# Decode attention over a 512 MiB cache: tiles of two heads with 64 KB runs in a ring of three slots

## The chip, the cores and the metric

The kernel runs on one core of a Trainium2 chip. The metric is the device time of one execution in microseconds (us); lower is better. A ratio is the mean time of one kernel's runs over the mean of the other's runs of the same rounds, so it is not quite the quotient of the medians that stand beside it. "Span" is the time from the first to the last instruction in the profile; it is about 2 us less than the device time.

Engines are named as in the profile: PE is the TensorE matmul, PEld its weight load, DVE is VectorE, ACT ScalarE, POOL GpSimd, SP SyncE. SPq and ACTq are the sequencers that issue DMA loads. "DMA engine" means one of the 16 hardware engines that move the bytes, not a queue.

## The reference, cut to what matters

```
# B=2, one query position, D=1024, H=32 heads, Sk=16384, Dh=128, bf16
g = sigmoid((x * gate_w).sum(-1))
q = x @ wq                                    # (B, H, Dh)
p = softmax(q . k_cache / sqrt(Dh))           # k_cache: (B, H, Sk, Dh), 256 MiB
a = (p . v_cache) @ wo                        # v_cache: 256 MiB
b = a small two-layer MLP branch of x with layernorms (w1, w2, w3, w4)
out = g * a + (1 - g) * b
```

The caches and weights are 572.5 MB (decimal), each byte of which is needed once. There is little arithmetic for each byte: the kernel is a stream of K and V tiles through on-chip memory.

## The kernel before: the parts that matter

Every K or V tile is one (batch, head) pair: 4 MB, 128 partitions with one contiguous run of 32 KB each. Five such slots form a ring. DVE transposes a K tile in eight pieces, PE multiplies them with a zero-padded q and collects scores in PSUM.

```python
big = ctx.enter_context(tc.tile_pool(name="big", bufs=5))      # 4 MB each
tpool = ctx.enter_context(tc.tile_pool(name="tpool", bufs=3))  # K transposed, 128x1024 f32
# ... other pools cut

def load_k(i):
    b, h = pairs[i]
    t = big_tile("Kn")
    nc.sync.dma_start(
        out=t[:].rearrange("p (j d) -> p j d", d=Dh),
        in_=A_k_cache[b, h].rearrange("(p j) d -> p j d", p=P),
    )
    kn_tiles[i] = t

x_pm = const.tile([P, B, KC], BF16)          # x by columns, pieces of 16 bytes
nc.scalar.dma_start(out=x_pm[:], in_=A_x.rearrange("b s (p r) -> p (b s) r", p=P))
x_row = rows.tile([B, D], BF16)
nc.scalar.dma_start(out=x_row[:], in_=A_x.rearrange("b s d -> (b s) d"))
# ... gate_w is loaded to two rows; the gate is computed on two partitions

def qk_stage(i):
    # ... cut
    for m in range(NM):                      # NM = 8
        T = tpool.tile([P, 2, CJ, 32], FP32, name="T")
        nc.vector.transpose(out=T[:].rearrange("p w j s -> p j w s"),
                            in_=Kw[:, m * CW : (m + 1) * CW].rearrange(...))
        for v in range(4):
            nc.tensor.matmul(S[:], lhsT=z[:, v, 7 - m : 7 - m + P],
                             rhs=Tb[:, v // 2, :, v % 2], start=..., stop=...)

# program order: q, gate, ln1, then for each pair: k, v of the pair before, softmax.
# A load is issued on the SP queue once the step that frees its slot has been built:
ring_size = {"big": 5, "wo": 3}
```

Of the kernel before, what the change touches and what calls it, by code (L numbers as in the profile page):

```python
# [10 lines left out]
FP32 = mybir.dt.float32  # L11
# [12 lines left out]
def kernel(  # L24
# [20 lines left out]
    assert Sq == 1 and Dh == P and B == 2  # L45
    NJ = Sk // P
    KC = D // P
    FC = F // P
    NM = 8
    CJ = NJ // NM  # L50
    NC_ = CJ * 32
    assert NC_ <= 512 and NJ == NM * CJ and D % 512 == 0
    scale = float(Dh) ** -0.5
    NPAIR = B * H
    SLOT = NJ * Dh
    W = 512
    DH2 = D // W

    const = ctx.enter_context(tc.tile_pool(name="const", bufs=1))
    big = ctx.enter_context(tc.tile_pool(name="big", bufs=5))  # L60
    tpool = ctx.enter_context(tc.tile_pool(name="tpool", bufs=3))
    wpool = ctx.enter_context(tc.tile_pool(name="wpool", bufs=3))
    ppool = ctx.enter_context(tc.tile_pool(name="ppool", bufs=2))
    stat = ctx.enter_context(tc.tile_pool(name="stat", bufs=3))
    rows = ctx.enter_context(tc.tile_pool(name="rows", bufs=1))
# [3 lines left out]
    mps = ctx.enter_context(tc.tile_pool(name="mps", bufs=3, space=PSUM))  # L69

    def misc_psum(shape, dtype):
        return mps.tile(shape, dtype, tag="misc", name="misc")
# [3 lines left out]


    pairs = [(b, h) for h in range(H) for b in range(B)]

    def load_rows(src, r0, rn, name):  # L80

        N = src.shape[1]
        t = big_tile(name)
        nc.sync.dma_start(
            out=t[:, : rn * N].rearrange("p (r n) -> p r n", n=N),
            in_=src.rearrange("(p r) n -> p r n", p=P)[:, r0 : r0 + rn, :],
        )
        return t[:, : rn * N].rearrange("p (r n) -> p r n", n=N)

# [3 lines left out]
    V_SPLIT_LAST = [NJ // 2, NJ // 4, NJ // 8, NJ // 8]  # L93

    def load_k(i):
        b, h = pairs[i]
        t = big_tile("Kn")
        nc.sync.dma_start(
            out=t[:].rearrange("p (j d) -> p j d", d=Dh),
            in_=A_k_cache[b, h].rearrange("(p j) d -> p j d", p=P),  # L100
        )
        kn_tiles[i] = t

    def load_v(i):
        b, h = pairs[i]
        t = big_tile("Vn")
        tv = t[:].rearrange("p (j d) -> p j d", d=Dh)
        src = A_v_cache[b, h].rearrange("(p j) d -> p j d", p=P)
        j0 = 0
        for n in V_SPLIT_LAST if i == NPAIR - 1 else [NJ]:  # L110
            nc.sync.dma_start(out=tv[:, j0 : j0 + n, :], in_=src[:, j0 : j0 + n, :])
            j0 += n
        vn_tiles[i] = t

    def load_wo(h):
        t = wpool.tile([P, D], BF16, tag="woh", name="woh")
        nc.sync.dma_start(out=t[:], in_=A_wo[h * Dh : (h + 1) * Dh, :])
        wo_tiles[h] = t

    x_pm = const.tile([P, B, KC], BF16)  # L120
    with nc.allow_non_contiguous_dma(reason="4 KB"):
        nc.scalar.dma_start(out=x_pm[:], in_=A_x.rearrange("b s (p r) -> p (b s) r", p=P))
    x_row = rows.tile([B, D], BF16)
    nc.scalar.dma_start(out=x_row[:], in_=A_x.rearrange("b s d -> (b s) d"))
    gw_row = rows.tile([B, D], BF16, tag="tmp_bf")
    for b in range(B):
        nc.scalar.dma_start(out=gw_row[b : b + 1, :], in_=gate_w.rearrange("(o d) -> o d", o=1))


    ident_bf = const.tile([P, P], BF16)  # L130
    make_identity(nc, ident_bf[:])
# [4 lines left out]
    quarter_f = const.tile([P, P], FP32)  # L136
    nc.vector.memset(quarter_f[:], 0.25)
    nscale_f = const.tile([1, P], FP32)
    nc.vector.memset(nscale_f[:], -scale)

    selv = const.tile([P, 4, 4, 32], BF16)
# [12 lines left out]
    own = const.tile([P, 16], BF16)  # L154
    nc.vector.memset(own[:], 0.0)
    for a in range(4):
        nc.vector.memset(own[32 * a : 32 * a + 32, 4 * a : 4 * a + 4], 1.0)

    assert CJ == 16
    osel = const.tile([P, 4], FP32)  # L160
    nc.vector.tensor_copy(out=osel[:], in_=ident_f[:, 0:8:2])
    for g in range(1, 4):
        nc.vector.tensor_tensor(
            out=osel[:], in0=osel[:], in1=ident_f[:, 40 * g : 40 * g + 8 : 2], op=ALU.add
        )
    ZW = P + 8
    NZ = 3
# [8 lines left out]


    pre_row = rows.tile([B, D], FP32)
    g_row = const.tile([B, 1], FP32)
    omg_row = const.tile([B, 1], FP32)  # L180

    def compute_gate():
        prod = pre_row
        nc.vector.tensor_tensor(out=prod[:], in0=x_row[:], in1=gw_row[:], op=ALU.mult)
        z = stat.tile([B, 1], FP32, name="z")
        nc.vector.reduce_sum(out=z[:], in_=prod[:], axis=AX.X)
        th = stat.tile([B, 1], FP32, name="zt")
        nc.scalar.activation(out=th[:], in_=z[:], func=ACTF.Tanh, scale=0.5)
        nc.vector.tensor_scalar(
            out=g_row[:], in0=th[:], scalar1=0.5, scalar2=0.5, op0=ALU.mult, op1=ALU.add  # L190
        )
        nc.vector.tensor_scalar(
            out=omg_row[:], in0=th[:], scalar1=-0.5, scalar2=0.5, op0=ALU.mult, op1=ALU.add
        )


    qT = const.tile([P, H, B], BF16)
    qsel = const.tile([P, NPAIR, 4], BF16)

    def compute_q():  # L200
        q_f = const.tile([P, H, B], FP32)
        for half in range(2):
            qps = misc_psum([P, H, B], FP32)
            rn = KC // 2
            for h in range(H):
                for r in range(rn):
                    nc.tensor.matmul(  # L207
                        qps[:, h, :],
                        lhsT=wq_half[half][:, r, h * Dh : (h + 1) * Dh],
                        rhs=xT[:, half * rn + r, :],  # L210
                        start=(r == 0),
                        stop=(r == rn - 1),
                    )
            if half == 0:
                nc.vector.tensor_copy(out=q_f[:], in_=qps[:])
            else:
                nc.vector.tensor_tensor(out=qT[:], in0=q_f[:], in1=qps[:], op=ALU.add)
        qs_ps = misc_psum([P, 4, NPAIR], FP32)
        for v in range(4):
            nc.tensor.matmul(  # L220
                qs_ps[:, v],
                lhsT=selv[:, v].rearrange("p a w -> p (a w)"),
                rhs=qT[:].rearrange("p h b -> p (h b)"),
                start=True,
                stop=True,
            )
        nc.vector.tensor_copy(out=qsel[:], in_=qs_ps[:].rearrange("p v n -> p n v"))

    def build_z(i):
        if i >= NPAIR:  # L230
            return
        z = z_tiles[i % NZ]
        nc.gpsimd.tensor_tensor(  # L233
            out=z[:, :, 7 : 7 + P].rearrange("p v (x e) -> p v x e", e=8)[:, :, :, 0],
            in0=qsel[:, i, :].unsqueeze(2).to_broadcast([P, 4, 16]),
            in1=own[:].unsqueeze(1).to_broadcast([P, 4, 16]),
# [5 lines left out]
    wo_acc = [acc.tile([B, W], FP32, name=f"wo_acc{n}") for n in range(DH2)]  # L242
# [4 lines left out]
    def qk_stage(i):  # L247
        Kw = kn_tiles.pop(i)[:].bitcast(FP32)
# [3 lines left out]
        CW = CJ * Dh // 2  # L252
        for m in range(NM):
            T = tpool.tile([P, 2, CJ, 32], FP32, name="T")
            nc.vector.transpose(  # L255
                out=T[:].rearrange("p w j s -> p j w s"),
                in_=Kw[:, m * CW : (m + 1) * CW].rearrange("p (j w e) -> p j w e", w=2, e=32),
            )
            Tb = T[:].rearrange("p w j s -> p w (j s)").bitcast(BF16).rearrange(
                "p w (n two) -> p w n two", two=2  # L260
            )
            for v in range(4):
                nc.tensor.matmul(  # L263
                    S[:],
                    lhsT=z[:, v, 7 - m : 7 - m + P],
                    rhs=Tb[:, v // 2, :, v % 2],
                    start=(m == 0 and v == 0),
                    stop=(m == NM - 1 and v == 3),
                )

    def softmax_stage(i):
# [3 lines left out]
        mT = misc_psum([1, P], FP32)  # L275
        nc.tensor.transpose(mT[:], m[:], ident_f[:])
        mx = stat.tile([1, 1], FP32, name="mx")
        nc.vector.reduce_max(out=mx[:], in_=mT[:], axis=AX.X)  # L278
        nb_ps = misc_psum([P, 1], FP32)
        nc.tensor.matmul(nb_ps[:], lhsT=nscale_f[:], rhs=mx[:], start=True, stop=True)  # L280
        nb = stat.tile([P, 1], FP32, name="nb")
        nc.vector.tensor_copy(out=nb[:], in_=nb_ps[:])  # L282
        Pr = ppool.tile([P, NC_], BF16, name="Pr")
# [4 lines left out]
        PT = ppool.tile([P, CJ, 32], BF16, name="PT")  # L288
        nc.vector.transpose(out=PT[:].rearrange("p j m -> p (j m)"), in_=Pr[:])  # L289
# [3 lines left out]
    def pv_rows(V, PT, oc):  # L293
# [4 lines left out]
        for m in range(NM):  # L298
            lhsT = PT[:].rearrange("p j m -> p (j m)")[:, m : CJ * 32 : 16]
            for g in range(4):  # L300
# [3 lines left out]
                    lhsT=lhsT,  # L304
# [4 lines left out]
        Os = rows.tile([P, 4, Dh], FP32, name="Os")  # L309
# [284 lines left out]
```

## Time and profile before

| | |
|---|---|
| device time | 1348.2 us |
| span of the profiled run | 1346.0 us |
| HBM read | 572.5 MB |
| rate from 150 to 1300 us | 430 GB/s |
| 572.5 MB at that rate | 1331 us |

First, lines of the profile's page: the busy time of each engine, the busy tenths of the 16 DMA engines and their GB/s in 40 slices of the span, the queue of instruction fetches (packets, MB, share of the DMA engines), the chain that ended last by engine, and the group of the K transposes (busy us, mean ns | idle before, what ended most of it).

```profile
PE 955.1 (71%) x5716; PEld 452.2 (34%) x5716; DVE 743.6 (55%) x954; ACT 88.4 (7%) x195; POOL 34.4 (3%) x79
...
DMA  9999999999999999999999999999999999999996
GB/s 405 427 431 431 432 429 430 431 430 432 426 430 432 431 429 428 432 433 430 426 433 432 429 429 429 433 429 431 427 429 430 433 428 430 430 433 429 428 431 293
...
q14 instruction: 15, 0.12, 0.0%
...
DMA 61%; PE 26%; DVE 8%; issue 2%; ACT 1%; DVEq 0%; POOL 0%; ACTq 0%
...
L255 DVE STREAM_TRANSPOSE T<-Kn 128x1024 f32<-128x1024 f32 x512 | 596.1, 1216 | 114.7 <-DMA Kn<-in_A_k_cache_dram 89.9
```

No compute engine is near full, DMA is at 9 tenths or more in 39 of 40 slices, and the last chain is mostly DMA. So the kernel is bound by DMA: only the speed of the packets, a gap in their stream, and the head and tail of the run can change the time.

The view of DMA issues (size, us from issue to landing) and the timeline of the start (start us, duration, engine, instruction [idle before it <- what ended it]) show the head:

```profile
x_pm<-in_A_x_dram ACTq DMA_DIRECT2D x1, 4.0 KB, 22.0
```

```profile
22.77 0.17 DVE L175 COPY xT<-x_pm 128x16 bf16<-128x16 bf16 x1 [20.32 <-DMA x_pm<-in_A_x_dram]
...
34.30 9.36 DVE L255 STREAM_TRANSPOSE T<-Kn 128x1024 f32<-128x1024 f32 x8
```

The 4 KB of x take 22 us, because they come in 256 pieces of 16 bytes on the ACT queue while the SP queue streams big packets. The first K transpose begins at 34.3 us. With five slots there is enough in flight to cover that.

The table of windows (window, length, then busy us and count of PE, PEld, DVE, ACT, POOL, then granted clock, DMA share, GB/s) for the start, the middle and the end:

```profile
core 0: us, PE busy (x) PEld busy (x) DVE busy (x) ACT busy (x) POOL busy (x), PEclk, DMA share, GB/s
80.00:92.00 12.00, 8.11 (x25) 3.28 (x26) 8.89 (x9) 0.55 (x2) 0.00 (x0) 0.59 1.00 425
110.00:120.00 10.00, 8.62 (x65) 4.24 (x63) 4.72 (x7) 0.80 (x2) 0.49 (x1) 0.98 0.98 421
150.00:1300.00 1150.00, 829.49 (x4719) 389.37 (x4718) 637.03 (x805) 76.56 (x170) 27.27 (x56) 0.75 1.00 430
1334.00:1338.00 4.00, 2.32 (x15) 1.96 (x16) 1.37 (x5) 0.82 (x3) 0.00 (x0) 0.72 0.56 231
1338.00:1342.00 4.00, 3.69 (x129) 3.52 (x129) 0.23 (x2) 0.00 (x0) 0.00 (x0) 0.50 0.20 76
```

There is no gap at the start, and at the end the share of busy DMA engines falls from full to nothing within about 10 us.

### The profile page before, as it was taken

Reading aid. Unit: us, or ns where it says so; the run is one execution under the profiler, and the core shown is the slowest. Engines: PE = TensorE matmul, PEld = TensorE weight load, DVE = VectorE, ACT = ScalarE, POOL = GpSimd, SP = SyncE. Lnnn points to the kernel's source line nnn. Section 1 sums busy time; section 2 is a strip of 40 time slices with the busy share of each in tenths; the row PEclk is TensorE's granted clock in tenths of the full one; section 3 lists DMA queues with packets and bytes.
Section 4 is the critical chain, followed back from the end, with each engine's and each line's share of the span. In section 5 each row is a group of like instructions: output and inputs, shape, how many; then the busy total and the mean of one; then the engine's idle time right before and its main releaser. Section 6 shows DMA issues by size and latency. Waiting matters only on the chain.

```text
span 1346.0 us, 13528 instructions
## 1 busy us (share of the span) xinstructions
PE 955.1 (71%) x5716; PEld 452.2 (34%) x5716; DVE 743.6 (55%) x954; ACT 88.4 (7%) x195; POOL 34.4 (3%) x79
## 2 busy tenths in 40 slices
PE   2777677677767766777667687767766766876776
PEld 2333333333333324333223233333333333333333
DVE  2756546456636653656526536655655665664564
ACT  0000000000000000000000000000000000000000
POOL 0000000000000000000000000000000000000000
PEclk9887677778877776887778778778777777777877
DMA  9999999999999999999999999999999999999996
GB/s 405 427 431 431 432 429 430 431 430 432 426 430 432 431 429 428 432 433 430 426 433 432 429 429 429 433 429 431 427 429 430 433 428 430 430 433 429 428 431 293
DMA packets 24967, 573.39 MB, mean 426 GB/s; under 512 B 3014, under 2 KB 3014, under 8 KB 7372
## 3 DMA queue, kind: packets, MB, share of 16 engines
q1 hardware_dynamic: 24628, 572.54, 99.3%
q8 instruction: 44, 0.72, 0.2%
q14 instruction: 15, 0.12, 0.0%
q10 hardware_dynamic: 280, 0.01, 0.0%
HBM read 572.53 MB, written 0.00 MB: 425 GB/s over the span
## 4 chain that ended last, share of the span: by engine, by line
DMA 61%; PE 26%; DVE 8%; issue 2%; ACT 1%; DVEq 0%; POOL 0%; ACTq 0%
DMA Kn<-in_A_k_cache_dram 37%; DMA Vn<-in_A_v_cache_dram 22%; PE S L263 14%; DVE T L255 6%; PE O L302 5%; PE misc L433 2%; DMA x_pm<-in_A_x_dram 2%; PE misc L312 2%; PE misc L407 1%; ACT Pr L285 1%; DVE PT L289 1%; ACT Os L310 1%; PE misc L207 1%; PE misc L280 0%; PE misc L318 0%
## 5 line engine op out<-in xcount | busy, mean ns | idle before, releaser
L255 DVE STREAM_TRANSPOSE T<-Kn 128x1024 f32<-128x1024 f32 x512 | 596.1, 1216 | 114.7 <-DMA Kn<-in_A_k_cache_dram 89.9
L263 PE MATMUL S<-T,z_136 128*128 128x512 bf16 x704 | 208.6, 458 | 58.4 <-DVE T L255 57.1
L263 PE MATMUL S<-T,z_138 128*128 128x512 bf16 x672 | 199.5, 460 | 66.4 <-DVE T L255 65.8
L263 PE MATMUL S<-T,z_140 128*128 128x512 bf16 x672 | 201.7, 465 | 57.7 <-DVE T L255 57.4
L302 PE MATMUL O<-Vn,PT 128*32 128x512 bf16 x2016 | 133.3, 410 | 40.0 <-DMA Vn<-in_A_v_cache_dram 40.0
L337 DVE TENSOR_SCALAR OT<-misc,rinv 128x1 bf16<-128x1 f32 x64 | 14.1, 221 | 246.1 <-PE misc L312 242.6
L263 PEld LDWEIGHTS <-z_136 128*128 128x128 bf16 x704 | 81.7, 116 | 180.3 <-issue 125.7
L263 PEld LDWEIGHTS <-z_138 128*128 128x128 bf16 x672 | 78.7, 117 | 183.5 <-issue 132.7
L263 PEld LDWEIGHTS <-z_140 128*128 128x128 bf16 x672 | 79.3, 118 | 176.4 <-issue 126.4
L302 PEld LDWEIGHTS <-PT 128*32 128x32 bf16 x2016 | 69.9, 143 | 100.5 <-DMA Vn<-in_A_v_cache_dram 48.0
L312 PE MATMUL misc<-osel,Os 128*128 128x1 f32 x504 | 69.6, 259 | 47.2 <-ACT Os L310 47.2
L310 ACT COPY Os<-O 128x512 f32<-128x512 f32 x63 | 36.9, 585 | 994.5 <-PE O L302 994.5
L312 PEld LDWEIGHTS misc<-osel,Os 128*128 128x128 f32 x504 | 64.2, 200 | 78.4 <-ACT Os L310 78.4
L274 DVE TENSOR_REDUCE m<-S 128x1 f32<-128x512 f32 x64 | 44.3, 693 | 74.4 <-PE S L263 74.4
L332 PE MATMUL misc<-rs,quarter_f 128*128 128x1 f32 x128 | 35.8, 349 | 67.0 <-ACT Pr L285 67.0
L289 DVE STREAM_TRANSPOSE PT<-Pr 128x512 bf16<-128x512 bf16 x64 | 45.4, 709 | 50.3 <-ACT Pr L285 50.3
L285 ACT ACTIVATE Pr<-S,nb 128x512 bf16<-128x512 f32 x64 | 44.0, 687 | 224.1 <-DVE nb L282 224.1
L332 PEld LDWEIGHTS misc<-rs,quarter_f 128*128 128x128 f32 x128 | 30.7, 297 | 72.7 <-ACT Pr L285 72.3
L280 PE MATMUL misc<-mx,nscale_f 1*128 1x1 f32 x128 | 28.3, 288 | 13.8 <-DVE mx L278 13.8
L280 PEld LDWEIGHTS misc<-mx,nscale_f 1*128 1x128 f32 x128 | 22.8, 221 | 36.7 <-DVE mx L278 36.7
L282 DVE COPY nb<-misc 128x1 f32<-128x1 f32 x64 | 10.1, 157 | 45.1 <-PE misc L280 45.1
L233 POOL TENSOR_TENSOR z_136<-qsel,own 128x64 bf16<-128x64 bf16 x22 | 10.7, 487 | 431.8 <-PE S L263 424.9
(85 smaller groups left out, 232.1 us busy)
## 6 DMA issues: line engine op xcount, KB each, us to landing
Kn<-in_A_k_cache_dram SPq DMA_DIRECT2D x64, 4096.0 KB, 46.1
Vn<-in_A_v_cache_dram SPq DMA_DIRECT2D x63, 4096.0 KB, 39.3
wt<-in_B_w_dram SPq DMA_DIRECT2D x4, 3584.0 KB
woh<-in_A_wo_dram SPq DMA_DIRECT2D x32, 256.0 KB, 39.0
wq_161<-in_A_wq_dram SPq DMA_DIRECT2D x1, 4096.0 KB, 12.2
wq_163<-in_A_wq_dram SPq DMA_DIRECT2D x1, 4096.0 KB, 21.7
wt<-in_B_w_dram SPq DMA_DIRECT2D x2, 2048.0 KB
Vn<-in_A_v_cache_dram SPq DMA_DIRECT2D x1, 2048.0 KB
```

Source lines behind the costliest of these rows:

```text
L255: nc.vector.transpose(out=T[:].rearrange("p w j s -> p j w s"), in_=Kw[:, m * CW : (m + 1) * CW].rearrange("p (j w e) -> p j w e", w=2, e=32),
L263: nc.tensor.matmul(S[:], lhsT=z[:, v, 7 - m : 7 - m + P], rhs=Tb[:, v // 2, :, v % 2], start=(m == 0 and v == 0), stop=(m == NM - 1 and v ...
L274: nc.vector.reduce_max(out=m[:], in_=S[:], axis=AX.X)
L280: nc.tensor.matmul(nb_ps[:], lhsT=nscale_f[:], rhs=mx[:], start=True, stop=True)
L285: nc.scalar.activation(out=Pr[:], in_=S[:], func=ACTF.Exp, bias=nb[:], scale=scale, accum_out=rs[:])
L289: nc.vector.transpose(out=PT[:].rearrange("p j m -> p (j m)"), in_=Pr[:])
L302: nc.tensor.matmul(O[32 * g : 32 * g + 32, :], lhsT=lhsT, rhs=V[:, j0 : j0 + 4, :], start=(m == 0), stop=(m == NM - 1),)
L310: nc.scalar.copy(out=Os[:].rearrange("p x d -> p (x d)"), in_=O[:])
L312: nc.tensor.matmul(oc[:], lhsT=Os[:, x, :], rhs=osel[:, x : x + 1], start=(x == 0), stop=(x == 3))
L332: nc.tensor.matmul(tot_ps[:], lhsT=quarter_f[:], rhs=rs[:], start=True, stop=True)
L337: nc.vector.tensor_scalar(out=OT[:, h, b : b + 1], in0=oc[:], scalar1=rinv[:, 0:1], scalar2=None, op0=ALU.mult)
L433: nc.tensor.matmul(dst[n][:], lhsT=actT[:, r0 + r, :], rhs=w[:, r, n * W : (n + 1) * W], start=(first and r == 0), stop=(last and r == rn ...
```

## The change

Its intent is fewer and larger DMA packets: a tile holds two neighbouring heads, so that each partition reads one run of 64 KB. To fit, the ring shrinks from five slots of 4 MB to three of 8 MB, and the buffers for transposed K from three of 128x1024 to two of 128x512. Scores, softmax and outputs work on two heads at once, which halves their number. The gate and the MLP branch work on columns (all 128 partitions) instead of rows. The diff, cut to its core:

```diff
-    big = ctx.enter_context(tc.tile_pool(name="big", bufs=5))
-    tpool = ctx.enter_context(tc.tile_pool(name="tpool", bufs=3))
+    big = ctx.enter_context(tc.tile_pool(name="big", bufs=NBIG))      # NBIG = 3, 8 MB each
+    tpool = ctx.enter_context(tc.tile_pool(name="tpool", bufs=2))
 ...
     def load_k(i):
-        b, h = pairs[i]
         t = big_tile("Kn")
         nc.sync.dma_start(
-            out=t[:].rearrange("p (j d) -> p j d", d=Dh),
-            in_=A_k_cache[b, h].rearrange("(p j) d -> p j d", p=P),
+            out=t[:].rearrange("p (j d) -> p j d", d=Dh), in_=cache_rows(A_k_cache, i)
         )
 ...
     x_pm = const.tile([P, B, KC], BF16)
+    gw_pm = const.tile([P, KC], BF16)
         nc.scalar.dma_start(out=x_pm[:], in_=A_x.rearrange("b s (p r) -> p (b s) r", p=P))
-    x_row = rows.tile([B, D], BF16)
-    nc.scalar.dma_start(out=x_row[:], in_=A_x.rearrange("b s d -> (b s) d"))
-    gw_row = rows.tile([B, D], BF16, tag="tmp_bf")
-    for b in range(B):
-        nc.scalar.dma_start(out=gw_row[b : b + 1, :], in_=gate_w.rearrange("(o d) -> o d", o=1))
+        nc.scalar.dma_start(out=gw_pm[:], in_=gate_w.rearrange("(p r) -> p r", p=P))
 ...
     def compute_gate():
-        prod = pre_row
-        nc.vector.tensor_tensor(out=prod[:], in0=x_row[:], in1=gw_row[:], op=ALU.mult)
+        prod = const.tile([P, B, KC], FP32, name="prod")
+        nc.vector.tensor_tensor(
+            out=prod[:], in0=x_pm[:], in1=gw_pm[:].unsqueeze(1).to_broadcast([P, B, KC]), op=ALU.mult
+        )
 ...
         for m in range(NM):                                  # NM: 8 -> 16, for two heads
-            T = tpool.tile([P, 2, CJ, 32], FP32, name="T")
-            nc.vector.transpose(... whole, 128x1024 ...)
-            for v in range(4):
-                nc.tensor.matmul(...)
+            for wh in range(2):
+                T = t_tile([P, CJ, 32], FP32)
+                nc.vector.transpose(out=T[:], in_=Kw[:, m * CJ : (m + 1) * CJ, wh, :])
+                for par in range(2):
+                    nc.tensor.matmul(...)
 ... softmax of two heads at once, output of two heads at once, MLP by columns: cut ...
-    ring_size = {"big": 5, "wo": 3}
+    ring_size = {"big": NBIG, "wo": 1, "T": G}
```

One thing that the diff alone does not show is the order of DVE's instructions. DVE runs its program in order. In the built kernel the copy of x, then `prod` (which waits for the gate load `gw_pm`), come ahead of the copies of q that the scores need and ahead of the first K transposes. And DVE's program grows from 1344 to 2373 instructions, counted in the built programs with the register and semaphore instructions that the profile does not count: two half transposes stand where one whole one stood.

## The prediction

> **What bounds the kernel now.** DMA. The slice row shows the 16 DMA engines at 9 tenths or more in 39 of 40 slices, 430 GB/s inside (the window table: 430 GB/s and a DMA share of 1.00 from 120 to 1300 us). The kernel reads 572.5 MB, 1331 us at that rate; the rest of the 1346 us span is a 2 us start, a 6 us tail after the last V piece, and slower ends. PE (71%) and DVE (55%) are not the limit: in the chain of waits most of the time is K and V loads.
>
> **What the change does.** Same bytes. K and V packets of 64 KB instead of 32 KB (a row per partition is now one run). In the packet records a 32 KB packet takes 1216 ns (median), 16 KB 614 ns: about 12 ns fixed plus the bytes. Halving 16,512 packets on 16 engines saves an estimated 6 to 10 us, if a 64 KB run really is one packet. Softmax and output work, halved in count, is off the critical path. w4 by columns costs PE 224 loads and matmuls of about 60 ns for 56 of about 300: the same.
>
> **What it puts at risk: the ring.** Three 8 MB slots instead of five of 4 MB.
> 1. Start. The x load is 16-byte pieces on another queue, 16 per DMA engine. In the timeline it lands only at 22 us: in the packet records, one 16-byte packet passes after each 1.22 us K packet. The Trainium skill (DMA: Bandwidth & Descriptors, Queues, rings and completion order) says that an engine round-robins between queues by packet; this trace agrees. With 64 KB packets (estimate 2.42 us) x lands at about 42 us and the new gate load behind it, 8 pieces per engine, at about 63. The built order of DVE puts the gate product, which waits for it, before the copies that lead to q and before the first K transposes. So they start near 66 us (34 before). K0's slot comes free near 93, but the DMA queue (wq, K0, K1, V0) ran dry at 80; V1 waits likewise for K1. Estimate: 10 to 15 us idle twice, before K2 and before V1.
> 2. Pace. A half transpose is about 0.71 us (128x512 bf16: 709 ns). With two T buffers each pair of buffers costs transpose + two matmuls + about 0.1 us: 0.71 us per half at full clock, 0.93 at half (granted clock mean 0.76), so 26 to 27 us for K's 32 halves, 4.5 for outputs, 5.5 for the softmax chain: 37 of the 39.5 us that the DMA needs per K and V. It holds, with little to spare.
> 3. Tail about the same (5 to 7 us).
>
> **Sum:** 1348 - 8 + 25 (start) - 1 to + 4 = about 1364 us, 1343 to 1388. Faster by 2% is impossible in practice (the DMA floor is above 1321): 0.01. Within 2%: 0.76. Slower by 2%: 0.23.
>
> **What the profile would show.** Right: packets of 65536 B near 2.42 us; 432 to 433 GB/s in middle slices; x landing near 42 us, the first transpose near 66; two dips of DMA in the third and fourth slices, DMA at 9 tenths after. Transposes of about 0.7 us.
>
> **What would make it wrong.** If runs are cut into 32 KB packets, x lands at 22 us, gate at 33, no start stall and no saving: 1346 to 1352. If small packets don't wait longer behind large ones, the saving stays: about 1340. If the work per tile exceeds 39.5 us, each of 32 tiles adds the excess, and it goes beyond 1390.

## More of the kernel before

Runs e1 to e9 were made on three chips (e1 to e4, e5 to e7, and e8 with e9). The kernel before ran beside each group, with medians of 1348.53, 1348.25 and 1348.10 us, so a difference between runs of different groups is uncertain by about 0.4 us. The lines of the profile's page shown in this section are those of the kernel before.

## The result, and the profile after

| | before | after |
|---|---|---|
| device time, median of 4 runs | 1348.18 us | 1369.95 us |
| lowest and highest | 1348.01, 1348.26 | 1369.56, 1370.39 |
| ratio, 95% interval | | 1.0162 [1.0144, 1.0179] |
| rate from 150 to 1300 us | 430 GB/s | 431 GB/s |

All outputs are right. The changed kernel is 1.6% slower. That is within the 2% that count as "same" here, but the 21.8 us are real: the four runs of each kernel here lie within 0.9 us of each other.

Lines of the page of the changed kernel, the same as shown of before:

```profile
PE 901.4 (66%) x5707; PEld 401.5 (29%) x5770; DVE 783.3 (57%) x1373; ACT 45.0 (3%) x99; POOL 14.3 (1%) x45
...
DMA  9967999999999999999999999999999999999995
GB/s 422 434 280 336 428 426 430 434 426 438 426 436 434 434 425 434 428 432 436 435 430 432 434 432 430 432 428 432 430 434 427 431 428 429 432 426 434 431 414 230
...
q14 instruction: 23, 0.18, 0.0%
...
DMA 53%; PE 26%; DVE 16%; another core or an unknown queue 2%; issue 2%; ACT 1%; SPq 0%; ACTq 0%
...
L284 DVE STREAM_TRANSPOSE T<-Kn 128x512 f32<-128x512 f32 x1024 | 688.3, 701 | 220.6 <-DMA Kn<-in_A_k_cache_dram 152.7
```

DMA has two dips, in the third and fourth slice (280 and 336 GB/s), and is full from then on. So the kernel is still bound by DMA, but with a gap near the start. The last slice is also emptier than before (230 against 293 GB/s).

The small loads in the view of DMA issues (other issues left out), and the timeline from the start to the second gap, with one line of the tail:

```profile
x_pm<-in_A_x_dram ACTq DMA_DIRECT2D x1, 4.0 KB, 41.4
...
gw_pm<-in_gate_w_dram ACTq DMA_DIRECT2D x1, 2.0 KB, 61.7
```

```profile
42.12 0.17 DVE L195 COPY xT<-x_pm 128x16 bf16<-128x16 bf16 x1 [39.85 <-DMA x_pm<-in_A_x_dram]
...
63.01 0.17 DVE L213 TENSOR_TENSOR prod<-x_pm,gw_pm 128x16 f32<-128x16 bf16 x1 [20.71 <-DMA gw_pm<-in_gate_w_dram]
...
65.93 1.30 DVE L284 STREAM_TRANSPOSE T<-Kn 128x512 f32<-128x512 f32 x2
...
89.54 0.33 SPq L97 DMA_DIRECT2D Kn<-in_A_k_cache_dram  x1
...
117.49 0.33 SPq L108 DMA_DIRECT2D Vn<-in_A_v_cache_dram  x1
...
1362.62 0.59 PE L350 MATMUL misc<-PT,Vn 128*128 128x2 bf16 x16 [0.48 <-DMA Vn<-in_A_v_cache_dram]
```

x lands at 42 us, the gate weights at 63 us, and only then can DVE go on to q and to the first transpose at 65.9 us (34.3 before). The slot of the first K tile is free when its last transposes are done, so the third K tile (L97) is issued at 89.5 us; the second V tile (L108) waits likewise for the second K tile, until 117.5 us. The waits of the DMA queue between 30 and 135 us say the same (us in total, times, longest):

```profile
SPq L97 <- DVE T L284: 36.9, 1, 36.9
...
SPq L108 <- DVE T L284: 27.5, 1, 27.5
```

The windows, as for before, and at the end of the run:

```profile
80.00:92.00 12.00, 9.00 (x31) 2.92 (x30) 9.93 (x17) 0.00 (x0) 0.33 (x1) 1.00 0.26 88
110.00:120.00 10.00, 8.97 (x60) 3.51 (x62) 7.63 (x12) 0.00 (x0) 0.34 (x1) 1.00 0.29 105
150.00:1300.00 1150.00, 783.03 (x4663) 344.87 (x4717) 679.89 (x1171) 38.69 (x86) 10.83 (x30) 0.82 1.00 431
1350.00:1354.00 4.00, 1.99 (x18) 1.63 (x16) 1.03 (x5) 1.08 (x3) 0.00 (x0) 0.97 0.53 205
1354.00:1358.00 4.00, 2.82 (x92) 2.85 (x93) 0.99 (x3) 0.18 (x2) 0.00 (x0) 0.50 0.06 27
1358.00:1362.00 4.00, 4.00 (x156) 4.00 (x153) 0.00 (x0) 0.00 (x0) 0.00 (x0) 0.50 0.10 29
```

Two things are to be seen. First, the two gaps: DMA is busy for a quarter of the windows at 80 and 110 us that were full before. Summed over the packet records from 20 to 200 us, the DMA engines are idle for 18.35 us. Secondly, the tail: from 1354 us on the DMA share is 0.06, which is one engine of 16. One DMA engine goes on alone until 1362 us, and the last matmuls wait for what it brings.

The packet records (each packet's start, duration, queue and bytes, which the trace holds beside its views) give the two other quantities of the argument:

| packet | count | median ns | mean ns |
|---|---|---|---|
| before, 32768 bytes | most of K and V | 1216 | 1220 |
| after, 65536 bytes | 8192 | 2420 | 2432 |

Two packets of 32 KB take 2440 ns, one of 64 KB 2432: about 8 ns less. That is little, and the rate in the middle of the run rose only from 430.1 to 431.0 GB/s by those records. And while the big packets stream, sixteen 16-byte packets, as many as there are DMA engines, pass in every 2.42 us now and in every 1.22 us before: one for each big packet. The Trainium skill ("DMA: Bandwidth & Descriptors", section "Queues, rings and completion order") says that a DMA engine serves its queues in turn, a whole packet at a time; this trace agrees, with the intervals just given. The page typically counts 9 to 17 descriptors to a packet; here a turn of the small queue was a single piece of 16 bytes.

### The profile page after: what moved, and what is told of

It is laid out like the page before. It is cut to its first block, busy times and chain, and to the rows that moved or that the text cites. A ratio compares the mean times of both kernels' runs of the same rounds, so it can differ in the third digit from the quotient of the medians. Undisturbed runs are those within 1.5% of the kernel's fastest.

```text
span 1367.8 us, 14339 instructions
## 1 busy us (share of the span) xinstructions
PE 901.4 (66%) x5707; PEld 401.5 (29%) x5770; DVE 783.3 (57%) x1373; ACT 45.0 (3%) x99; POOL 14.3 (1%) x45
## 4 chain that ended last, share of the span: by engine, by line
DMA 53%; PE 26%; DVE 16%; another core or an unknown queue 2%; issue 2%; ACT 1%; SPq 0%; ACTq 0%
DMA Kn<-in_A_k_cache_dram 46%; PE S L289 19%; DVE T L284 15%; PE O L333 4%; DMA Vn<-in_A_v_cache_dram 4%; DMA x_pm<-in_A_x_dram 3%; PE misc L343 1%; PE wo_acc L379 1%; ACT Os L341 1%; PE misc L200 1%; ACT Pr L317 0%; DVE PT L321 0%; DVE OT L371 0%; DVE mx L310 0%
## 5 line engine op out<-in xcount | busy, mean ns | idle before, releaser
L284 DVE STREAM_TRANSPOSE T<-Kn 128x512 f32<-128x512 f32 x1024 | 688.3, 701 | 220.6 <-DMA Kn<-in_A_k_cache_dram 152.7
L289 PE MATMUL S<-T,z_135 128*128 128x512 bf16 x992 | 328.4, 419 | 142.9 <-DVE T L284 130.9
L289 PE MATMUL S<-T,z_137 128*128 128x512 bf16 x993 | 325.2, 414 | 144.7 <-DVE T L284 131.8
L289 PEld LDWEIGHTS <-z_135 128*128 128x128 bf16 x1024 | 107.0, 104 | 361.4 <-issue 308.1
L289 PEld LDWEIGHTS <-z_137 128*128 128x128 bf16 x1024 | 106.4, 104 | 360.1 <-issue 305.9
L343 PE MATMUL misc<-osel,Os 128*128 128x2 f32 x248 | 32.7, 254 | 12.6 <-ACT Os L341 11.2
L431 PEld LDWEIGHTS <-wt 128*128 128x128 bf16 x576 | 35.9, 169 | 16.4 <-DMA wt<-in_B_w_dram 15.1
L321 DVE STREAM_TRANSPOSE PT<-Pr 128x512 bf16<-128x512 bf16 x32 | 22.7, 711 | 28.7 <-ACT Pr L317 28.7
L343 PEld LDWEIGHTS misc<-osel,Os 128*128 128x128 f32 x248 | 30.0, 191 | 21.1 <-ACT Os L341 21.1
L300 DVE TENSOR_REDUCE m<-S 128x1 f32<-128x512 f32 x32 | 22.2, 692 | 22.5 <-PE S L289 22.5
L317 ACT ACTIVATE Pr<-S,nb 128x512 bf16<-128x512 f32 x32 | 22.0, 688 | 122.1 <-DVE nb L312 119.1
L379 PEld LDWEIGHTS <-woh 128*128 128x128 bf16 x256 | 20.7, 168 | 10.4 <-issue 10.2
L237 PEld LDWEIGHTS <-wt 128*128 128x128 bf16 x256 | 7.1, 104 | 45.0 <-DMA wt<-in_A_wq_dram 22.7
```

The lines of the kernel that those rows point to most:

```text
L237: nc.tensor.matmul(qps[:, h, :], lhsT=wq[:, r, h * Dh : (h + 1) * Dh], rhs=xT[:, r, :], start=(r == 0), stop=(r == KC - 1),)
L284: nc.vector.transpose(out=T[:], in_=Kw[:, m * CJ : (m + 1) * CJ, wh, :])
L289: nc.tensor.matmul(S[:], lhsT=z[:, 2 * wh + par, NM - 1 - m : NM - 1 - m + P], rhs=Tb[:, :, par], start=(m == 0 and wh == 0 and par == 0), ...
L300: nc.vector.reduce_max(out=m[:], in_=S[:], axis=AX.X)
L317: nc.scalar.activation(out=Pr[:], in_=S[:], func=ACTF.Exp, bias=nb[:], scale=scale, accum_out=rs[:])
L321: nc.vector.transpose(out=PT[:], in_=Pr[:])
```

## The experiments

The theory that the prediction leaves: the late start (small loads behind 64 KB packets, with DVE in order behind them) costs some 20 us, and the larger packets give some back. Rivals: the two small transpose buffers are too slow for the pace all along; the loss is in the tail; or the larger packets themselves give nothing. The first four runs separate these.

### e1: the small loads first

The loads of x and of the gate weights are issued on the SP queue, ahead of all the big loads.

```diff
-        nc.scalar.dma_start(out=x_pm[:], in_=A_x.rearrange("b s (p r) -> p (b s) r", p=P))
-        nc.scalar.dma_start(out=gw_pm[:], in_=gate_w.rearrange("(p r) -> p r", p=P))
+        nc.sync.dma_start(out=x_pm[:], in_=A_x.rearrange("b s (p r) -> p (b s) r", p=P))
+        nc.sync.dma_start(out=gw_pm[:], in_=gate_w.rearrange("(p r) -> p r", p=P))
```

> The changed kernel with the two small loads (x and the gate weights) issued first on the queue of the big loads. Theory (late start behind 64 KB packets): both small loads land by about 4 us, q starts when wq has landed (about 23 us), the first K transpose at about 34 us, no DMA gap before K2 or V1; 18.7 us of idle DMA vanish, so about 1351 us. Rival (the ring of three 8 MB slots cannot feed the DMA however early it starts): gaps of over 5 us stay, 1360 us or more.

Measured: 1351.66 us, ratio to before 1.0024 [1.0009, 1.0039]. The view of DMA issues has x landing 1.7 us after its issue; the first transpose begins at 44.4 us, when the first K tile has landed. The window that had the first gap, two of the tail, and the page's line of instruction fetches:

```profile
80.00:92.00 12.00, 10.13 (x34) 3.27 (x34) 11.85 (x18) 0.00 (x0) 0.00 (x0) 1.00 0.99 427
1334.00:1338.00 4.00, 1.32 (x20) 1.16 (x21) 1.65 (x6) 0.78 (x2) 0.00 (x0) 0.78 0.20 81
1338.00:1342.00 4.00, 4.00 (x156) 4.00 (x154) 0.00 (x0) 0.00 (x0) 0.00 (x0) 0.50 0.08 30
```

```profile
q14 instruction: 22, 0.18, 0.0%
```

The gap is gone and 18.3 us with it, close to the idle time that was measured in the changed kernel (18.35 us). The match is not exact: in its first 20 us e1 has 0.8 us more idle time than the changed kernel (e6 mends that), and it has one fetch of instructions less (see the tail, below). So the late start is most of the loss, and the pace of the transposes is not the matter: with the same two small buffers there is no other gap. But e1 is still slower than before, and the tail with one lone DMA engine (share 0.08 from 1338 us) is still there.

### e2: the gate after the second softmax

The loads stay late; only the gate's work on DVE is moved out of the way of q and the first K tile. (`prod` lies in a shared buffer so that the order is kept.)

```diff
-        prod = const.tile([P, B, KC], FP32, name="prod")
+        prod = ppool.tile([P, B, KC], FP32, tag="PrOs", name="prod")
 ...
-    steps = [("q", compute_q), ("gate", compute_gate)]
+    steps = [("q", compute_q)]
 ...
             steps.append(("", lambda i=i: softmax_stage(i + 1)))
+        if i == 0:
+            steps.append(("gate", compute_gate))
```

> The changed kernel with the gate's work placed behind the second tile's softmax, x still loaded late (about 42 us). Theory: the first K transpose moves from 66 to about 54 us; K0 is used up near 78 us, just before the DMA runs dry at 80.5, so the first gap (10.0 us) vanishes; K1 is used up near 105.5 us while K2 has landed at 100, so a second gap of about 6 to 7 us stays: about 1358 us. If the gate's load has no part in it, 1370.

Measured: 1356.84 us, ratio 1.0063 [1.0046, 1.0079]. The first transpose begins at 53.1 us instead of 65.9. Two windows:

```profile
80.00:92.00 12.00, 9.76 (x29) 3.40 (x29) 9.60 (x17) 1.59 (x3) 0.00 (x0) 0.72 1.02 438
100.00:107.00 7.00, 6.36 (x48) 2.60 (x50) 5.03 (x8) 0.00 (x0) 0.33 (x1) 1.00 0.44 150
```

The first gap is gone, and of the second 5.9 us are left. The gate's place in DVE's program cost 13.1 us (1369.95 less 1356.84), the late x alone 5.2 us (1356.84 less e1's 1351.66). So x itself is late enough to harm a ring of three, and the gate load behind it is the larger part.

### e3 and e4: runs of 32 KB again

Every load with runs of 64 KB is issued as two with runs of 32 KB; e3 from the changed kernel, e4 from e1.

```diff
-        nc.sync.dma_start(
-            out=t[:].rearrange("p (j d) -> p j d", d=Dh), in_=cache_rows(A_k_cache, i)
-        )
+        tk = t[:].rearrange("p (j d) -> p j d", d=Dh)
+        src = cache_rows(A_k_cache, i)
+        for a in range(2):
+            sl = slice(a * NJ // 2, (a + 1) * NJ // 2)
+            nc.sync.dma_start(out=tk[:, sl, :], in_=src[:, sl, :])
 ... the same for V and the weights
```

> The changed kernel with every 64 KB run loaded as two loads of 32 KB runs: same ring, same slots, same order, packets of 32 KB. Theory: x lands near 22 us and the gate load near 33, first K transpose near 36, no gap; the packets cost 2 to 4 us more in all: about 1354 us. Rival (the ring itself): still 1365 or more.

> Both: early x and 32 KB packets. Against the run with early x alone it measures what packets of 64 KB are worth by themselves, with no start stall in either. From the packet records (2 x 1220 ns against 2432 ns, 8192 packets on 16 engines): 4 us slower than with 64 KB packets; if the last engine to finish decides instead, anything within 5 us either way.

Measured: e3 1357.03 us, ratio 1.0064 [1.0049, 1.0079], 3 us more than expected; e4 1357.74 us, ratio 1.0070 [1.0055, 1.0085]. In e3 x, on the ACT queue, lands as early as in the kernel before and the gate weights behind it, as the view of DMA issues shows, and the window has no gap:

```profile
x_pm<-in_A_x_dram ACTq DMA_DIRECT2D x1, 4.0 KB, 22.1
...
gw_pm<-in_gate_w_dram ACTq DMA_DIRECT2D x1, 2.0 KB, 32.5
```

```profile
80.00:92.00 12.00, 10.86 (x88) 4.39 (x87) 8.12 (x12) 0.00 (x0) 0.34 (x1) 1.00 1.02 437
```

So the size of the big packets is what made the small loads late: apart from it, only the number of big loads issued differs between e3 and the changed kernel. With 32 KB packets it makes no odds whether the small loads are early (e4 is 0.7 us slower than e3). And the large packets do give something: e4 is 6.1 us slower than e1, more than the 4 us that the packet durations had led me to expect (8 ns for each of 8192 packets over 16 engines).

What is left: e3 and e4 have neither a gap nor the gain of large packets, and are still some 9 us slower than the kernel before. All four runs have the lone DMA engine at the end.

### The tail: two theories

From the packet records I took, for each kernel, the time at which four or more DMA engines were last busy with packets of 4 KB or more of the cache and weight loads, and the time at which the last such packet ended:

| kernel | fetch packets on q14 | four engines busy until | last packet ends | difference |
|---|---|---|---|---|
| before | 15 | 1339.3 | 1339.8 | 0.5 |
| after | 23 | 1352.5 | 1362.1 | 9.6 |
| e1 | 22 | 1334.6 | 1344.1 | 9.5 |
| e4 | 23 | 1339.8 | 1349.3 | 9.5 |

(The counts of fetch packets are the profile's own; in the changed kernel's, one packet has 96 bytes, so that 22 have 8 KB.) The kernels with half transposes have one DMA engine 9.5 us behind the others. What else is different about them? q14 is a queue of instruction fetches: packets of 8 KB, 325 ns each, one for about every 128 instructions of DVE (1029 more instructions, 8 more packets). At the end of the changed kernel, where the lone engine's packets can be told apart, the records show one such fetch between V packets of 4 KB that otherwise take 160 ns:

| start us | ns | queue | bytes |
|---|---|---|---|
| 1359.55 | 160 | loads | 4096 |
| 1359.70 | 332 | q14, instructions | 8192 |
| 1360.02 | 499 | loads | 4096 |
| 1360.50 | 31 | loads | 4 |
| 1360.52 | 476 | loads | 4096 |
| 1360.99 | 160 | loads | 4096 |

The fetch and the slower packets around it cost that engine about 1.0 us (332 for the fetch, 499 and 476 less the usual 160 each, and some 20 for the packet of 4 bytes). Theory A: DVE's fetches all ride on one DMA engine; eight or nine more of them put it 8 to 9 us behind, and since each tile has rows from every engine, the last tile lands that much later. Theory B: the half transposes make the last K tile slow to finish (22.9 us from its first to its last transpose, in the median tile), and the end of the run waits for that.

### e5: whole transposes again

From e1: transposes of 128x1024 in two buffers of that size. Room is made by keeping the softmax's and the output's scratch tiles in those same buffers, by one z tile instead of two, and by loading the last two `wo` tiles into a big slot. DVE's program falls from 2373 to 1317 instructions.

```diff
-            for wh in range(2):
-                T = t_tile([P, CJ, 32], FP32)
-                nc.vector.transpose(out=T[:], in_=Kw[:, m * CJ : (m + 1) * CJ, wh, :])
+            T = t_tile([P, 2, CJ, 32], FP32)
+            nc.vector.transpose(
+                out=T[:].rearrange("p w j s -> p j w s"), in_=Kw[:, m * CJ : (m + 1) * CJ]
+            )
 ...
-    NZ = 2
+    NZ = 1
 ...
-        mdiag = ppool.tile([P, P], FP32, tag="PrOs", name="mdiag")
+        mdiag = t_tile([P, P], FP32, "mdiag")
 ... the same for Pr and Os; the last two wo tiles in a big slot: cut
```

> Early x, and K transposed in whole instructions of 128x1024 again (two T buffers of 4 KB; to make room mdiag, Pr and Os take T buffers, one z tile, the last two wo tiles take a big slot). DVE's program falls from 2373 to 1317 instructions. Theory (instruction fetches of DVE ride on one DMA engine that also carries K and V; with twice the instructions that engine ends about 10 us after the others): 8 KB fetch packets inside the run fall from 21 to about 12, the last DMA engine ends 4 to 6 us closer to the others, K of the last tile is done about 4 us sooner (about 19 us instead of 23): 1345 to 1348 us. Rival (the late engine has another cause and only it sets the end): 1350 to 1352, as with early x alone.

Measured: 1342.90 us, ratio 0.9960 [0.9947, 0.9972]: 8.8 us faster than e1, more than expected, and faster than the kernel before. The lone engine is gone: four engines are busy until 1335.0 us, and the last packet ends at 1335.5. By itself this does not decide between A and B, because several buffers changed and a K tile became quicker (19.5 us from its first to its last transpose in e6, which has the same transposes).

### e6: the weights of q first

From e5: the two small loads go behind wq on the same queue instead of ahead of it, so that the head of the run has no small packets.

```diff
+    load_rows(["wq"], [A_wq])
     x_pm = const.tile([P, B, KC], BF16)
 ...
-    xfers = [("big", "q", lambda: load_rows(["wq"], [A_wq]))]
+    xfers = [("big", "q", lambda: None)]
```

> As the run with whole transposes, but the two small loads stand behind wq in the same queue instead of ahead of it: they then land with wq (about 22 us) and do not delay the start of the stream, which in the run with early x lost 0.75 us at the head (idle share of the DMA engines in the first 20 us: 0.94 against 0.19 us). 0.5 to 1 us less than the run with whole transposes. If the order at the head does not matter: equal within 0.3 us.

Measured: 1342.11 us, ratio 0.9954 [0.9940, 0.9968]. That is 0.8 us better than e5, and the fastest of all. The end of this kernel, by windows and by the page's line of fetches:

```profile
1330.00:1334.00 4.00, 3.22 (x110) 3.05 (x109) 0.00 (x0) 0.00 (x0) 0.00 (x0) 0.50 0.56 218
1334.00:1338.00 4.00, 1.89 (x40) 1.78 (x36) 0.56 (x3) 0.00 (x0) 0.00 (x0) 0.50 0.13 48
1338.00:1342.00 4.00, 0.00 (x0) 0.00 (x0) 0.00 (x0) 0.00 (x0) 0.00 (x0) 0.50 0.04 1
```

```profile
q14 instruction: 13, 0.11, 0.0%
```

### e7: e6 with DVE's program made longer

This is the control for e5. Whole transposes stay, all buffers stay, and two copies of one element per partition are added after each K transpose, except in the last K tile, so that nothing near the end is slower. They do nothing but add instructions: DVE's program grows from 1317 to 2280. Theory A expects the lone engine back, B no change.

```diff
+    pad = const.tile([P, 8], FP32, name="pad")
 ...
+            for d in range(2 if i < NT - 1 else 0):
+                nc.vector.tensor_copy(out=pad[:, (2 * m + d) % 8 : (2 * m + d) % 8 + 1], in_=T[:, d, 0, 0:1])
```

> As the run with wq first, with two tiny copies (128x1) on DVE behind each K transpose except in the last tile: 963 more instructions on DVE (2280), no other work and no wait that matters (DVE keeps 10 us and more free per tile). Theory of the fetches: about 8 more 8 KB fetch packets, one DMA engine ends 6 to 8 us later than in the run without, and the time rises by 4 to 8 us. Rival (the number of DVE instructions has no part in it): equal within 1 us.

Measured: 1349.76 us, ratio 1.0011 [0.9998, 1.0023]: 7.65 us slower than e6. Lines of the page (fetches; the added copies) and the windows of the end:

```profile
q14 instruction: 21, 0.17, 0.0%
...
L292 DVE COPY pad<-T 128x1 f32<-128x1 f32 x992 | 83.9, 139 | 2.1
```

```profile
1334.00:1338.00 4.00, 2.73 (x102) 2.65 (x100) 0.00 (x0) 0.00 (x0) 0.00 (x0) 0.50 0.14 53
1338.00:1342.00 4.00, 3.14 (x110) 2.97 (x107) 0.00 (x0) 0.00 (x0) 0.00 (x0) 0.50 0.08 30
1342.00:1346.00 4.00, 1.79 (x36) 1.68 (x33) 0.57 (x3) 0.00 (x0) 0.00 (x0) 0.50 0.02 9
```

The lone engine is back (share 0.08 from 1338 us): by the packet records four engines are busy until 1333.8 us and the last packet ends at 1342.3, 8.5 us later, against 1334.0 and 1334.4 in e6. The other engines are done when they were done in e6. Eight more fetch packets, 7.65 us: theory A's figure. B falls, as the last K tile has no added copies. The copies' own 84 us of DVE time are spread over the whole run, where DVE has time to spare.

### e8: the best one with 32 KB runs

e6 with every load of 64 KB runs split in two, the edit of e3.

> The fastest version so far (whole transposes, small loads behind wq, 1342.1 us) with every 64 KB run loaded as two loads of 32 KB runs. If the gain over the kernel before comes from the packets alone, it rises by about 6 us (as between the two runs with early x, 1351.7 and 1357.7) to about 1348 us, level with the kernel before. If the two-head tiles are worth something by themselves it stays below 1345.

Measured: 1347.89 us, ratio 0.9999 [0.9985, 1.0013]. The large packets are worth 5.8 us in the best kernel, as they were worth 6.1 in e1. And everything else in e6, two heads at a time and the columns, is in sum worth nothing: e8 is the kernel before to within 0.3 us.

### e9: whole transposes, small loads late

e5 with the small loads on the ACT queue again, the edit of e1 undone.

> The changed kernel with whole transposes alone, the small loads late as in the change. Theory: the late start stays (first transpose near 66 us), but a K tile is used up in about 19 instead of 24 us, so the two gaps shrink from 18.7 to about 10 or 11 us, and the late DMA engine saves about 9 us as it did with early x: about 1353 us. If the two causes were one, whole transposes alone would bring back most of it (1345) or little (1365).

Measured: 1357.21 us, ratio 1.0067 [1.0054, 1.0081]: 14.3 us slower than e5, and 4 us more than expected. Its two gaps in the windows:

```profile
80.00:90.00 10.00, 7.47 (x29) 2.69 (x27) 8.12 (x11) 0.00 (x0) 0.33 (x1) 1.00 0.32 106
106.00:116.00 10.00, 9.12 (x58) 3.68 (x59) 8.37 (x9) 0.00 (x0) 0.34 (x1) 1.00 0.33 111
```

By the packet records the DMA engines are idle for 13.9 us in all, more than the 10 to 11 I had worked with, and this again is the loss against e5. The quicker K tiles free the slots sooner, so the gaps are 4.4 us shorter than in the changed kernel. The lone engine is not there (1348.5 and 1349.8 us). The two faults of the change are thus independent: each was repaired without the other, and what each repair gained is what its trace had shown as lost.

## Why the prediction was right or wrong, point by point

The time of 1364 us was 6 us short, inside its range, and "within 2%" was right. The steps of it, with what the runs give for each (the prediction does not name its "-1 to +4"; it is taken here for the tail):

| term | predicted | measured | from |
|---|---|---|---|
| larger packets | -8 | -5.8 | e6 against e8 |
| late start | +25 | +18.3 | after against e1 |
| tail | -1 to +4, "about the same" | +8.8 | e1 against e5 |
| small loads at the head (e1's place for them) | not in it | +0.8 | e5 against e6 |
| two heads, columns, softmax | 0 | -0.3 | e8 against before |
| sum | +16 to +21 | +21.8 | |

The pairs form one chain from before to after (before, e8, e6, e5, e1, after), so the measured terms must add up to the measured difference: the sum is no test of them. What tests the late start and the tail are the traces, 18.35 us of idle DMA engines in the one case and a last engine 9.5 us behind in the other.

- **Right: what bounds the kernel, and the mechanism of the start.** x landed at 42.1 us ("about 42"), the gate weights at 63.0 ("about 63"), the first transpose began at 65.9 ("near 66"), the dips came in the third and fourth slices, and e3 shows that the size of the packets is the cause, e2 and e1 that DVE's order and the late x carry it on to the DMA queue.
- **Right in kind, too large in size: the start.** I had the first K tile's slot free at 93 us and two gaps of 10 to 15 us; it was free at 89.5, because a K tile took about 24 us and not 26 to 27. I had costed the matmuls at a reduced clock. In the windows of the gaps the granted clock is 1.00, so the half transposes (701 ns in the mean, 0.71 predicted) set the pace.
- **Right: the pace holds.** From 120 us to the tail the DMA engines are idle for 0.16 us in all.
- **Right in kind, too large: the packets.** 2420 ns against the estimate of 2.42 us, and one packet for each run. But 431 GB/s were measured in the middle, not 432 to 433, and 5.8 us of the 6 to 10.
- **Wrong: the tail.** "Tail about the same (5 to 7 us)", and -1 to +4 us in the sum. It cost 8.8 us. I had looked at what DVE's and PE's instructions take, and had not counted how many there are: twice as many instructions for DVE mean twice as many fetches, these are DMA packets too, and DVE's all lie on one DMA engine (shown below). Of the 8.8 us between e5 and e1, where buffers changed as well, e7 shows 7.65 by added instructions alone. The page of the kernel before already showed this queue (15 packets). The start, costed 6.7 us too high, hid most of this error, so that the closeness of the total is partly luck.

The Trainium skill ("Runtime: NRT & Kernel Launch", section "Instruction fetch mechanics") says that the cost of crossing into the next block of instructions is "mostly hidden". Hidden or not for DVE, which was not looked into, a fetch is not hidden for the DMA engine that carries the fetches of a kernel bound by DMA: about 1 us each.

**What the landing records add.** The packet records do not name the DMA engine of a packet. But the trace also holds, for each load, when each of its 16 DMA engines reported its share as landed; no view prints these times. In e4 the last of the 16 engines falls a further 0.95 to 1.02 us behind the first at 17 of the 23 fetches on q14. Two early fetches are partly or wholly hidden, as another engine was still the latest, and the other four move nothing. At the end the last engine is 9.15 us behind the second-last. One engine alone drifts away, so these 19 fetches all lie on it. In the middle of the run, too, the packet right behind such a fetch is stretched (1.87 us for 1.215 in e4, 3.08 for 2.42 in the changed kernel); with the 0.33 us of the fetch this makes the 1.0 us.

In each kernel three to five fetches on q14 are followed by a less stretched packet (1.57 to 1.71 us with 32 KB, 2.77 to 2.85 with 64 KB); in e4 these are the four that move nothing. Without them 10 fetches remain in before, e6, e8 and e9, 18 in e7, and 19 in after, e1 and e4, about what DVE's programs give at 128 instructions each. Whose the others are was not looked for. So three comparisons give nearly 1 us per fetch: 8.8 us for nine (e5 to e1), 7.65 for eight (e6 to e7), and 8.3 for nine (e9 to after, 12.7 us less the 4.4 us of longer gaps).

The same records show why ten fetches leave no lone engine. Each fetch of 16 KB on the other instruction queue, q8 (44 or 45 of them), puts one of eight other engines about 1.55 us behind, in turn (e8). At the last V load of e6 seven engines are done within 1.04 us; those eight and the one with DVE's fetches follow 7.8 to 9.7 us after the first. The kernel before has the same split (7.9 to 10.0 us), so the fetches make much of its tail of about 10 us too.

**What stays open.** Between e6 and e8 the packet records explain the gain of large packets: means of 2427.1 and 1219.6 ns, thus 12.1 ns less for each 64 KB and 6.2 us in all, for 5.8 measured. Between e1 and e4 the same reckoning gives 4.3 us of 6.1, and the rest is unexplained. No run changes the number of slots, so the part of the ring of three in the late start is argued and not measured. Whether DVE itself ever waits for a fetch was not looked into.

## What to carry to other kernels

In this kernel, bound by DMA, packets of twice the size on one queue made a small load on another queue nearly twice as late (41.4 us for 22.0): put small loads on the same queue where they are wanted, and keep what waits for them out of the way of the first work of an engine that runs in order. Count the instructions of each engine as well as their time: their fetches are DMA packets, and with 18 or 19 of DVE's the DMA engine that carried them decided when a tile had landed, while with 10 it was level with others. And undo the parts of a change singly: here a real gain of 5.8 us was buried under two side effects of 18 and 9 us, and with both repaired the version of e6 ran at 1342.11 us, 0.46% faster than the kernel before and 2% faster than the changed one.

## What the Trainium skill lacked or had wrong

- "DMA: Bandwidth & Descriptors", section "Queues, rings and completion order": the turn-taking by packets is right, but it puts typically 9 to 17 descriptors into a turn, where here one piece of 16 bytes passed, and a consequence is lacking, that large packets delay the small loads of other queues: 4 KB in 16-byte pieces landed after 22.0 us beside packets of 32 KB, after 41.4 us beside packets of 64 KB, and after 1.7 us when issued first.
- "Runtime: NRT & Kernel Launch", section "Instruction fetch mechanics": the fetch is called mostly hidden, which is said of the engine that fetches, and comes in blocks of 16 KiB. What it costs the DMA engines is lacking. The runs show packets of 8 KB on one queue (13 to 23, growing with DVE's program, about 128 instructions each) and of 16 KB on another (44 or 45). In this kernel, bound by DMA, a DVE fetch put one DMA engine about 1 us behind (7.65 us for eight more, e7), and a 16 KB fetch put one of eight others about 1.55 us behind.
- "CRC Debugging", section "Comparing the Two Runs", puts the instruction refills on queue 14. If the profile counts queues in the same way, that is incomplete: it shows two queues of instruction packets here, q8 (44 or 45 packets) and q14 (13 to 23).
- "DMA: Bandwidth & Descriptors", section "Where 436 GB/s comes from": for loads from HBM it lets a limit of about 358 GB/s bind, though it also reports 425 GB/s measured for 16 MB. This kernel, on one core, read 430 to 432 GB/s for over a millisecond, near the 435 that the page gives for the fabric; what its neighbours did is not recorded.
